# Making the low parts of the up weights on POOL instead of DVE, in an attention and feed-forward kernel

## The chip, the cores and the metric

The kernel runs on one core of one Trainium2 chip. The metric is device time in microseconds; lower is better. A core has several engines that work side by side, each on its own instructions in their order: PE (matmul), DVE, ACT and POOL (elementwise work), and SP (which here issues DMAs). They wait for each other through semaphores.

## The reference

Attention with a relative-position bias, then a gated feed-forward layer without a nonlinearity other than the product of its two up projections. Cut to what matters here:

```python
scores = scale * q @ k.T + bias            # B=8, H=8, S=576, D=64
attn = softmax(scores)
x = (attn @ v) -> (B*S, H*D)               # 4608 x 512

a = x @ w1                                 # 512 -> 1024, "up"
b = x @ w2                                 # 512 -> 1024, "up"
h = a * b @ w3                             # 1024 -> 1024
out = h @ w_out                            # 1024 -> 512
```

The feed-forward weights (w1, w2, w3, w_out) arrive as float64; the kernel sees them as pairs of 32-bit integers and makes float32 of them itself.

## The kernel before

**Split operands.** PE multiplies in a rounded format (fp32r). To keep accuracy, an operand is split into a high part, its rounded copy, and a low part, the difference of the operand and the high part. A product of two split operands is three matmuls: high by high, low by high, high by low. For the up weights the high part is `wh` (made by ACT, L579) and the low part is `wl` (made by DVE, L582).

**Stages.** First come a prologue (the bias table) and the attention, 32 units of one head pair and one batch each. In its last part, and overlapping its end, the kernel folds w3 and w_out into one matrix (`fold`, `evict_w`: L596 to L629). Then follow nine chunks of 512 tokens; in a chunk, eight steps `ft` of `up` (two groups of 12 matmuls, L661, into PSUM; ACT copies the first, DVE multiplies it with the second to `g`, ACT rounds it to `gh`, DVE makes `gl`) and `down` (12 matmuls with the folded matrix, L686). The up weights stay in SBUF for all chunks: they are made once.

**Up weights.** There are 16 tiles, for m = 0, 1 (w1, w2) and t = 0 to 7, each 128 x 512. This text numbers them n = 2t + m. `split_w` makes one, as a sequence of ten steps:

| step | line | engine | what |
|---|---|---|---|
| fetch | L123 | SP queue | DMA of the tile as integers to `wi` |
| size, rest | L128, L131 | ACT | `wmag` from the high words, `w` from the low words |
| clamp, shift, head, power | L134, L137, L143, L148 | DVE | bits of the float32 value in `wmag`, its power of two into `wi` |
| total | L151, L152 | POOL | `w` times the power, plus `wmag`: the float32 weight `w` |
| wh | L579 | ACT | the rounded copy |
| wl | L582 | DVE | `w` minus `wh` |

The pools give two buffers to `wi` and `wmag` and three to `w`, so the fetch of tile n + 2 waits until L151 of tile n has read its `wi`.

**Order.** The kernel writes the order of PE, ACT, DVE and POOL by hand: every step has a planned time, `drive` sorts the steps by it, and each engine gets its instructions in that order. Planned times are only keys for sorting. Tile n's steps stand at `AT_W1 + PACE_W * n` (4.0 and 5.7) after a base, plus the ten offsets in `AT_W`: total at +7.1, wh at +10.0, wl at +10.6. So on each engine wl of tile n stands between total of tile n and total of tile n + 1 (which is planned at +12.8).

```python
AT_W = 3.5, 0.0, 0.5, 1.2, 2.6, 3.8, 5.5, 7.1, 10.0, 10.6
```

**Neighbours in the same stretch.** The fold issues, for each of its 16 steps, an ACT rounding (`w3h`, L610), a DVE subtraction (`w3l`, L612) and 12 matmuls (L619); eight of the steps also have a POOL subtraction of the low part of w_out (L603, of the same form as wl: 128 x 512, fp32r from float32). `evict_w` has an ACT rounding and a DVE subtraction from PSUM (L626, L628). `split_x` splits the token chunk: DVE `xr` (L643), POOL `xh` (L647), DVE `xl` (L649). The first up steps bring DVE's `g` (L669, reads PSUM) and `gl` (L675). The up matmuls with `wl` (L661) of step t need both tiles n = 2t and n = 2t + 1.

Of the kernel before, what the change touches and what calls it, by code (L numbers as in the profile page):

```python
# [14 lines left out]
ALU = mybir.AluOpType  # L15
# [51 lines left out]
def relpos_attention_moe(  # L67
# [17 lines left out]
    nc = tc.nc  # L85
# [11 lines left out]
    def f(ap):  # L97
        return ap.bitcast(F32)
# [11 lines left out]
    def narrow(pool, src, n, x, queue, pieces=1):  # L110

        d = {}

        def cut(ap):
            return ap if pieces == 1 else ap.rearrange("p (c n) -> p c n", c=pieces)

        def fetch():
            if not WIDE:
                queue.dma_start(cut(x), src)
                return  # L120
            wi = pool.tile([P, n, 2], I32, name="wi")
            flat = wi.rearrange("p n t -> p (n t)")
            queue.dma_start(cut(flat), src.bitcast(I32))  # L123
            mag = pool.tile([P, n], F32, name="wmag")
            d.update(lo=wi[:, :, 0], hi=wi[:, :, 1], mag=mag, bits=mag.bitcast(I32), power=flat[:, 0:n])

        def size():
            nc.scalar.activation(d["mag"], f(d["hi"]), AF.Abs)  # L128

        def rest():  # L130
            nc.scalar.activation(x, d["lo"].bitcast(U32), AF.Copy, scale=2.0 ** -52)  # L131

        def clamp():
            nc.vector.tensor_scalar(d["mag"], d["mag"], LEAST, MOST, op0=ALU.max, op1=ALU.min)  # L134

        def shift():
            nc.vector.tensor_scalar(  # L137
                d["bits"], d["bits"], 3, 0x3FFFFFFF, op0=ALU.logical_shift_left, op1=ALU.bitwise_and,
            )

        def head():

            nc.vector.scalar_tensor_tensor(  # L143
                d["bits"], d["hi"], -0x40000000, d["bits"], op0=ALU.bitwise_and, op1=ALU.bitwise_or,
            )

        def power():
            nc.vector.tensor_scalar(d["power"], d["bits"], -0x800000, None, op0=ALU.bitwise_and)  # L148

        def total():  # L150
            nc.gpsimd.tensor_tensor(x, x, f(d["power"]), op=ALU.mult)  # L151
            nc.gpsimd.tensor_tensor(x, d["mag"], x, op=ALU.add)  # L152

        steps = [fetch, size, rest, clamp, shift, head, power, total]
        return steps if WIDE else [fetch] + [lambda: None] * 7
# [415 lines left out]
    def split_w(pool, t, m):  # L571
        src = (moe_w1, moe_w2)[m].rearrange("(c p) n -> p c n", p=P)[:, :, t * P:(t + 1) * P]
        w = cv.tile([P, NC * P], F32, name="w", bufs=3)
        for step in narrow(cv, src, NC * P, w, nc.sync, pieces=NC):
            step()
            yield
        w = w.rearrange("p (c n) -> p c n", c=NC)
        wh = pool.tile([P, NC, P], F32R, name=f"wh{m}{t}")
        nc.scalar.activation(wh, w, AF.Copy)  # L579
        yield  # L580
        wl = pool.tile([P, NC, P], F32R, name=f"wl{m}{t}")
        nc.vector.tensor_tensor(wl, w, f(wh), op=ALU.subtract)  # L582
        ups[m, t] = (wh, wl)

    def put_w(plan, pool, t, m, at):
        put(plan, split_w(pool, t, m), at - AT_W[0], *(at + d for d in AT_W[1:]))
# [149 lines left out]
    op = moe.enter_context(tc.tile_pool(name="op", bufs=NT))  # L736
# [73 lines left out]
```

## Time and profile before

| what | us |
|---|---|
| median of three runs (1241.46 to 1242.97) | 1242.62 |
| the profiled execution | 1243.18 |
| its span (first to last instruction) | 1241.4 |
| PE busy | 1200.8 |
| DVE busy | 656.6 |
| ACT busy | 603.5 |
| POOL busy | 390.0 |
| wl (L582), 16 instructions on DVE, starting from 603.7 to 702.9 | 11.3 |

The profile gives each instruction's engine, line, output and inputs, start and duration. Its views group instructions by line, list them in order of time, name what ended an engine's idle time (in brackets behind an instruction), and follow the chain that ended last back from the end. A duration is from an instruction's start on its engine to its end; where an instruction is held up after it has started, that shows as a longer duration, not as idle time. Starts of neighbours on DVE lie some 0.08 us closer than their durations say, since one begins while the one before it completes. The granted clock of PE is 0.989 over the span.

### The profile page before, as it was taken

The numbers are of one execution on the slowest core, as the hardware profiler recorded it, in microseconds if no ns is written. First come the engines' busy times: TensorE is split into PE (matmuls) and PEld (weight loads), VectorE is DVE, ScalarE is ACT, GpSimd is POOL, SyncE is SP. The second block draws the span as 40 slices with busy tenths as digits, with TensorE's granted clock in tenths as the row PEclk, the third lists the DMA queues.
The fourth block names the chain that finished last, engine by engine and source line by source line (L and its number), as shares of the span: only waits on it lengthen the run. The fifth ranks groups of instructions, "written<-read, shape, count | busy, mean of one in ns | idle before, by whom it ended". The sixth has DMA issues, their size and how long they took to land. (4 is left out here: it accounts for less than half of the span.)

```text
span 1241.4 us, 19015 instructions
## 1 busy us (share of the span) xinstructions
PE 1200.8 (97%) x7136; PEld 956.6 (77%) x7136; DVE 656.6 (53%) x1380; ACT 603.5 (49%) x1303; POOL 390.0 (31%) x260
## 2 busy tenths in 40 slices
PE   7679999999999999999989999999999999999998
PEld 3168887777778887887768788888888888888887
DVE  8647776777677767776999532222222131313111
ACT  7558887888788877888544321212121212121211
POOL 0436664666456655661654300000000000000000
PEclk9879999999999999999999999999999999999999
DMA  7854446444645463431443220212111110200001
GB/s 215 286 172 143 144 149 204 133 142 145 220 133 152 152 219 120 148 94 54 135 132 117 68 74 29 68 34 65 38 51 51 51 51 35 68 34 1 29 7 34
DMA packets 60795, 130.25 MB, mean 105 GB/s; under 512 B 8992, under 2 KB 18592, under 8 KB 60704
## 3 DMA queue, kind: packets, MB, share of 16 engines
q1 hardware_dynamic: 59408, 127.32, 32.7%
q10 hardware_dynamic: 1296, 1.72, 0.5%
q8 instruction: 56, 0.92, 0.3%
q14 instruction: 35, 0.29, 0.1%
HBM read 99.10 MB, written 29.92 MB: 104 GB/s over the span
## 5 line engine op out<-in xcount | busy, mean ns | idle before, releaser
L298 DVE CUSTOM_DVE_ANT_0 ts<-s,nb 128x576 f32<-128x576 f32 x256 | 184.7, 749 | 148.1 <-ACT pt L363 74.1
L661 PE MATMUL up<-xh,wl 128*128 128x512 f32 x576 | 225.4, 391 | 0.1
L669 DVE TENSOR_TENSOR g<-up,a 128x512 f32<-128x512 f32 x72 | 49.7, 690 | 332.2 <-PE up L661 332.2
L661 PE MATMUL up<-xh,wh 128*128 128x512 f32 x576 | 225.3, 391 | 0.0
L661 PE MATMUL up<-xl,wh 128*128 128x512 f32 x576 | 225.3, 391 | 0.0
L290 PE MATMUL s<-K,Q 128*128 128x288 f32 (+2 forms) x672 | 206.0, 326 | 16.2 <-DVE mx L298 7.6
L321 ACT ACTIVATE pp<-ts,mx 128x576 f32<-128x576 f32 x256 | 196.7, 770 | 39.2 <-DVE mx L298 39.1
L290 PE MATMUL s<-kl,Q 128*128 128x288 f32 (+2 forms) x672 | 182.1, 295 | 0.0
L686 PE MATMUL o<-w3s,gh 128*128 128x512 f32 x576 | 177.8, 390 | 0.0
L666 ACT COPY a<-up 128x512 f32<-128x512 f32 x72 | 42.2, 586 | 247.5 <-PE up L661 247.5
L647 POOL TENSOR_SCALAR xh<-xr 128x512 fp32r<-128x512 f32 x36 | 23.9, 664 | 435.7 <-DVE xr L643 432.5
L290 PEld LDWEIGHTS s<-K,Q 128*128 128x128 f32 x672 | 128.3, 191 | 38.2 <-DVE mx L298 18.0
L355 PE MATMUL pst<-ident,pp 128*128 128x128 f32 x1024 | 152.8, 278 | 0.0
L363 ACT ACTIVATE pt<-pst 128x512 f32<-128x512 f32 x224 | 129.5, 594 | 34.2 <-PE pst L355 29.9
L397 PE MATMUL pst<-pt,rv 128*64 128x320 f32 (+1 forms) x1024 | 138.3, 412 | 0.0
L355 PEld LDWEIGHTS pst<-ident,pp 128*128 128x128 f32 x1024 | 118.8, 141 | 15.2 <-DVE wi L148 11.8
L672 ACT ACTIVATE gh<-g 128x512 fp32r<-128x512 f32 x72 | 45.5, 632 | 172.8 <-DVE g L669 172.8
L290 PEld LDWEIGHTS s<-kl,Q 128*128 128x128 f32 x672 | 129.0, 192 | 0.0
L661 PEld LDWEIGHTS up<-xh,wl 128*128 128x128 f32 x576 | 108.2, 188 | 23.9 <-DVE wl L582 0.5
L661 PEld LDWEIGHTS up<-xl,wh 128*128 128x128 f32 x576 | 108.3, 188 | 23.3
L661 PEld LDWEIGHTS up<-xh,wh 128*128 128x128 f32 x576 | 108.3, 188 | 23.2
L686 PEld LDWEIGHTS o<-w3s,gh 128*128 128x128 f32 x576 | 108.2, 188 | 22.8
(85 smaller groups left out, 1720.3 us busy)
## 6 DMA issues: line engine op xcount, KB each, us to landing
rk<-in_k_dram SPq DMA_DIRECT2D x31, 576.0 KB
rq<-in_q_dram SPq DMA_DIRECT2D x31, 576.0 KB
wi<-in_moe_w_dram SPq DMA_DIRECT2D x32, 512.0 KB
nb_d<-bev SPq DMA_DIRECT2D x36, 295.5 KB
rv<-in_v_dram SPq DMA_DIRECT2D x32, 320.0 KB
x_d<-x SPq DMA_DIRECT2D x32, 288.0 KB
xr<-x_d SPq DMA_DIRECT2D x36, 256.0 KB
rb<-r_d SPq DMA_DIRECT2D x72, 128.0 KB
```

The costliest lines, as they stand in the source:

```text
L290: nc.tensor.matmul(o, l, r, start=(m == 0), stop=(m == len(ops) - 1))
L298: nc.vector.tensor_tensor_reduce(out=halves(ts), in0=d.pop(("s", t))[:, :, :HS], in1=halves(NB[p, t]), op0=ALU.add, op1=ALU.min, scale=-1. ...
L321: nc.scalar.activation(pp, ts, AF.Exp, bias=mx, scale=-1.0, accum_out=d["sum"][:, col:col + 1])
L355: nc.tensor.transpose(ps[:, c * P:(c + 1) * P], x, ident)
L363: nc.scalar.activation(o, x, AF.Copy)
L397: nc.tensor.matmul(acc[rows], x[:, c0:c0 + D], m, start=(c == 0), stop=(c == 4))
L647: nc.gpsimd.tensor_scalar(xh, xr, 1.0, 1.0, op0=ALU.mult, op1=ALU.mult)
L661: nc.tensor.matmul(acc, l[:, cc], r, start=(n == 0), stop=(n == 3 * NC - 1))
L666: nc.scalar.copy(a, ps[0])
L669: nc.vector.tensor_tensor(g, ps[1], a, op=ALU.mult)
L672: nc.scalar.activation(gh, g, AF.Copy)
L686: nc.tensor.matmul(d["o", t], l[:, sl], folded[ft][r], start=(ft == 0 and n == 0), stop=(ft == NF - 1 and n == 2),)
```

## The change

The subtraction that makes the low part of an up-weight tile is issued to POOL instead of DVE. Its planned time stays, so in POOL's order it stands behind total (L151, L152) of its own tile, and it waits there for ACT's `wh`.

```diff
@@ -579,7 +579,7 @@
         nc.scalar.activation(wh, w, AF.Copy)
         yield
         wl = pool.tile([P, NC, P], F32R, name=f"wl{m}{t}")
-        nc.vector.tensor_tensor(wl, w, f(wh), op=ALU.subtract)
+        nc.gpsimd.tensor_tensor(wl, w, f(wh), op=ALU.subtract)
         ups[m, t] = (wh, wl)
```

Nothing else is changed: tiles, buffers, planned times and the other engines' steps are the same.

## The prediction

> **What bounds the kernel now.** I read the page first, then the chain that ended last, then the stretch in which the edited line runs. The page: span, the busy tenths of DVE in 40 slices, and the chain by line.
>
> ```profile
> span 1241.4 us, 19015 instructions
> ...
> DVE  8647776777677767776999532222222131313111
> ...
> PE up L661 28%; PE o L686 14%; DVE wl L582 0%; DVE xr L643 0%; DVE wmag L143 0%; ACT osb L701 0%; DVE wmag L137 0%; POOL w L151 0%; POOL w L152 0%; ACT wh L579 0%; DVE gl L675 0%; DVE g L669 0%; ACTq L704 0%; ACT gh L672 0%; DVE xl L649 0%
> ```
>
> DVE reaches nine tenths in three slices only (about 590 to 683 us), and the chain that ended last, else PE's, passes through the small steps that prepare the up weights (wmag, w, wh, wl). The next view is that stretch, by windows (columns: length, then busy time and count of PE, PEld, DVE, ACT, POOL, then clock, DMA share, GB/s); the last row is the whole neighbourhood.
>
> ```profile
> 600.00:620.00 20.00, 19.73 (x90) 14.59 (x86) 19.90 (x22) 10.60 (x19) 13.22 (x10) 1.00 0.72 200
> 620.00:640.00 20.00, 15.59 (x64) 11.83 (x65) 19.96 (x27) 7.60 (x13) 10.10 (x8) 1.00 0.52 156
> 640.00:680.00 40.00, 40.00 (x176) 32.56 (x175) 39.01 (x51) 18.88 (x33) 19.72 (x15) 1.00 0.38 119
> 680.00:703.50 23.50, 22.64 (x99) 18.09 (x97) 18.76 (x28) 9.17 (x17) 12.49 (x10) 1.00 0.28 90
> 703.50:1241.40 537.90, 533.69 (x2340) 439.36 (x2339) 128.54 (x192) 96.69 (x166) 17.30 (x28) 1.00 0.13 42
> 590.00:720.00 130.00, 124.36 (x554) 97.55 (x553) 109.15 (x140) 56.63 (x100) 61.03 (x46) 1.00 0.38 116
> ```
>
> From 600 to 680 DVE is occupied 78.9 of 80 us. PE is idle 0.27 + 4.41 + 0 + 0.86 = 5.5 us between 600 and 703.5, and after that the kernel is PE alone for 537.9 us. So the end moves with the moment at which PE gets the last up weights. The chain around that moment, and, from the view of the waits between 580 and 760 us (total, times, longest), what PE waits for:
>
> ```profile
> 699.51 1.30 POOL w L151
> ...
> 702.85 0.70 DVE wl L582
> 703.55 0.04 issue
> 703.60 2.81 PE up L661 x11
> ```
> ```profile
> PE wacc L619 <- DVE w3l L612: 4.7, 3, 2.4
> ...
> PEld up L661 <- DVE wl L582: 0.5, 1, 0.5
> ```
>
> PE waits half a microsecond for the sixteenth low part, made at 702.85 to 703.55, and from there the chain is all PE but for the last output copy. There is therefore no slack at all: if the sixteen tiles come later, the end comes later by as much; if they come earlier, PE gains what it now idles, 5.5 us at the most.
>
> **The change: what goes from DVE.** Per tile one subtraction (L582). This is the tile numbered 5 of 0 to 15, in the timeline, ACT first, then POOL, then DVE:
>
> ```profile
> 641.41 0.63 ACT L579 ACTIVATE wh<-w 128x512 fp32r<-128x512 f32 x1 [2.81 <-POOL w L152]
> ```
> ```profile
> 644.06 1.30 POOL L151 TENSOR_TENSOR w<-w,wi 128x512 f32<-128x512 f32 x1 [2.68 <-issue]
> ```
> ```profile
> 641.69 0.69 DVE L143 SCALAR_TENSOR_TENSOR wmag<-wi,wmag 128x512 int32<-128x512 int32 x1
> 642.30 0.68 DVE L582 TENSOR_TENSOR wl<-w,wh 128x512 fp32r<-128x512 f32 x1
> 642.90 0.69 DVE L612 TENSOR_TENSOR w3l<-w3s,w3h 128x512 fp32r<-128x512 f32 x1
> 643.51 0.42 DVE L148 TENSOR_SCALAR wi<-wmag 128x512 int32<-128x512 int32 x1
> ```
>
> On a busy DVE the subtraction holds 642.90 - 642.30 = 0.60 us, so 16 of them give back 16 x 0.60 = 9.6 us of queue.
>
> **What comes to POOL, and what it does to DVE.** The kernel has POOL subtractions of the very same shape and types (L603). Here are two pairs of them in the same stretch, and the DVE instructions that lie beside them:
>
> ```profile
> 600.10 3.16 POOL L603 TENSOR_TENSOR wos<-wos,woh 128x512 fp32r<-128x512 f32 x2
> 607.89 3.18 POOL L603 TENSOR_TENSOR wos<-wos,woh 128x512 fp32r<-128x512 f32 x2
> ```
> ```profile
> 600.45 1.65 DVE L143 SCALAR_TENSOR_TENSOR wmag<-wi,wmag 128x512 int32<-128x512 int32 x1
> 602.03 1.78 DVE L612 TENSOR_TENSOR w3l<-w3s,w3h 128x512 fp32r<-128x512 f32 x1
> 608.14 1.78 DVE L612 TENSOR_TENSOR w3l<-w3s,w3h 128x512 fp32r<-128x512 f32 x1
> 609.85 1.77 DVE L143 SCALAR_TENSOR_TENSOR wmag<-wi,wmag 128x512 int32<-128x512 int32 x1
> ```
>
> Four POOL operations, four DVE operations of 1.65 to 1.78 us that take 0.68 to 0.69 us in the rows of tile 5, in POOL's idle 2.68 us. Each POOL subtraction cost DVE 0.97 to 1.10 us. That is more than the 0.60 us that leaves DVE. The groups of the whole stretch (590 to 720 us; count, busy time, mean ns) give the average, and show which operation does not suffer; the last row, one line's own view, gives the undisturbed time (minimum, median, maximum):
>
> ```profile
> L137 DVE TENSOR_SCALAR wmag<-wmag 128x512 int32<-128x512 int32 x16 | 17.0, 1063 | 0.3
> L134 DVE TENSOR_SCALAR wmag<-wmag 128x512 f32<-128x512 f32 x16 | 17.0, 1060 | 0.5 <-ACT wmag L128 0.5
> L143 DVE SCALAR_TENSOR_TENSOR wmag<-wi,wmag 128x512 int32<-128x512 int32 x16 | 15.7, 980 | 0.3
> L612 DVE TENSOR_TENSOR w3l<-w3s,w3h 128x512 fp32r<-128x512 f32 x15 | 15.1, 1003 | 1.6 <-ACT w3h L610 1.6
> L675 DVE TENSOR_TENSOR gl<-g,gh 128x512 fp32r<-128x512 f32 x9 | 9.3, 1037 | 2.0 <-ACT gh L672 1.8
> L669 DVE TENSOR_TENSOR g<-up,a 128x512 f32<-128x512 f32 x9 | 6.1, 682 | 8.6 <-PE up L661 8.6
> ```
> ```profile
> L134 DVE TENSOR_SCALAR wmag<-wmag x16: 414/1464/1524, 590.1 to 694.3; 128x512 f32<-128x512 f32 x16
> ```
>
> Over 0.41 us for L134 and L137 and 0.68 for the others, the excess is 16 x 0.65 + 16 x 0.65 + 16 x 0.30 + 15 x 0.32 + 9 x 0.36 = 33.6 us, beside 46 POOL operations (the count in the last window row): 0.73 us each on average (xh operations, which are shorter, among them). g, which reads one operand from PSUM, stays at 0.68 us. So the stall falls on DVE instructions with both inputs in SBUF and on the short tensor-scalar ones, and only while POOL works.
>
> The Trainium skill, page "SBUF — State Buffer", section "Who interferes with whom", speaks against the change: VectorE and GpSimd arbitrate for one pair of SBUF ports, and it is an exclusive lock held for the whole instruction. The rows above agree on which instructions suffer. Taken to the letter it would charge a whole POOL operation of about 1.28 us per tile, an estimate of 16 x (1.28 - 0.60) = 10.9 us; the rows show 0.2 to 0.3 us less per operation.
>
> **Where the POOL step stands.** In POOL's order it comes after its own tile's L152 and before the next tile's L151, a few times with an xh (L647) beside it. It waits for ACT's wh. In tile 5, wh ends at 642.04 and POOL has nothing until 644.06: a 1.3 us operation fits, so POOL's time as such is covered. Its port isn't. Step by step: POOL gets in when DVE's L143 is done (about 642.3) and holds to 643.6; w3l, next on DVE, is held off and ends near 644.2; L148 follows, near 644.55; L151 of the next tile, which needs L148, starts near 644.65 instead of 644.06. Shift: +0.6, against 1.10 - 0.60 = 0.50 by the rule of the rows. Behind the waiting wl stand L151, L152 and, in some tiles, xh on POOL, and through them ACT's wh, DVE's xl (which needs xh), and the weight fetch of two tiles on, since SP waits for L151 to free the buffer:
>
> ```profile
> SPq L123 <- POOL w L151: 56.3, 13, 7.5
> ```
>
> So the shift stays in the loop and is carried on. The tile w, now freed by POOL, has three buffers, so ACT needs it back three tiles later; that costs nothing. No DMA is issued by the moved step. I went through the timeline for the other tiles in this way. In twelve of the first fifteen the DVE instruction due when wh is ready is L148, w3l, xr, xl, L137 or a gl: price 0.50 each, 6.0 us. In three (tiles 2, 3 and 8) POOL meets evictions from PSUM, g, or a DVE that waits for xh anyway: I take 0.1 each, 0.3 us. The sixteenth has no successor; it lies itself on the chain, and takes about 1.3 us (L151 took 1.30 there) instead of 0.70: 0.6 us.
>
> **Sum.** 6.0 + 0.3 + 0.6 = 6.9, taken as +7 us. Bounds: with the average of 0.73 for all, 16 x 0.13 + 0.6 = 2.7 us; with 1.10 for all, 16 x 0.50 + 0.6 = 8.6 us. I stand near the upper one because the rows that are the same operation (L603) are those of 0.97 to 1.10. PE's present gaps do not cover it: 4.7 of the 5.5 us are waits for DVE's own w3l, which comes later too. The profiled execution took 1243.18 us, 1.8 more than its span; the median of the three runs is 1242.62. 1242.6 + 7 = 1249.6 us.
>
> **Rivals.**
>
> *DVE is really relieved (faster).* If POOL's operation mostly found DVE in PSUM work, or let DVE pass, a lock would cost less than 0.60 us, and below that the sign turns. At no cost DVE would be 9.6 us earlier, less 0.6 for the last tile; PE can take only the 5.5 us of its idle time, so 1237 us. For it: DVE is the fuller engine, and the new POOL step falls in POOL's idle time. Against it: the four L603 rows. The Trainium skill, page "Perfetto Trace Analysis", section "Optimizing Scalar/DVE Operations", says that moving work off a saturated DVE, even to GPSIMD, may make sense, and adds that for these two it might not help. Chance 0.10.
>
> *A wash.* A price near 0.60 to 0.7 us, the gain in the queue paid back by the lock: 1242 to 1245 us. The average of 0.73 lies close by. Chance 0.12 within 0.2% (2.5 us, about what a measurement of this kernel tells from no change), and 0.13 for a small loss of 2.5 to 4.5 us.
>
> *POOL's own queue becomes the bound.* Means of the rows in this stretch:
>
> ```profile
> L151 POOL TENSOR_TENSOR w<-w,wi 128x512 f32<-128x512 f32 x16 | 23.4, 1463 | 36.5 <-ACT w L131 17.7 <-issue 7.1 <-DVE wi L148 4.2
> ```
>
> L151 at 1.46, L152 of the same form at as much, ACT's 0.7 between, and the subtraction at 1.58 (half of 3.16) make 5.2 us a tile; from tile 5 to 15 the pitch of L151 is (699.51 - 644.06) / 10 = 5.5 us. It holds on average, with 0.3 us to spare, but xh and the pairs of L603 stand in the same queue. If this bites in half of the tiles by 0.5 us, 4 us come on top: 1253 to 1255 us. Chance 0.10.
>
> The forecast, 1247 to 1252, has the rest, 0.55. Slower by over 0.2%: 0.55 + 0.13 + 0.10 = 0.78; the same 0.12; faster 0.10. The range leaves a tenth on each side: 1242.5, which takes in the wash and the low bound, to 1254.5.
>
> **What would show it.** Right: wl on POOL sixteen times at 1.3 to 1.6 us; DVE's L148, now 0.42 us in tile 5, and w3l longer by about 1 us in most tiles; the last wl ending near 710 instead of 703.5; PE's idle time before it up by 7 us; the stretch behind it 538 us as before. Wrong: L148 still at 0.4 us and DVE with gaps (the relief), or DVE idle while POOL works back to back (POOL's queue). What would make the number wrong is above all the order in which the two engines get in: I assume that POOL waits for one DVE instruction and no more.

## The result: slower by half a per cent

| | kernel before | changed kernel |
|---|---|---|
| median of four runs each, us | 1242.75 (1241.46 to 1242.97) | 1248.80 (1248.24 to 1250.01) |
| the profiled execution, us | 1243.18 | 1249.16 |
| its span, us | 1241.4 | 1247.2 |

The ratio is 1.0052 [1.0037, 1.0067], a loss of 6.05 us. The forecast was +7 us, 1249.6 us.

**The page after.** The span, the busy tenths of DVE and of POOL in 40 slices of about 31 us:

```profile
span 1247.2 us, 19031 instructions
...
DVE  8647776777677767775989622222212231313111
...
POOL 0436664666466655661766500000000000000000
```

DVE is still in its eights and nines between 590 and 690 us, although sixteen instructions have left it: what the subtraction gave back was taken up again.

**The stretch before the last up weights**, in the windows view (length, then busy time and count of PE, PEld, DVE, ACT, POOL, then clock, DMA share, GB/s); the last row is again 590 to 720:

```profile
600.00:620.00 20.00, 18.99 (x84) 13.94 (x79) 19.90 (x18) 9.80 (x18) 16.93 (x12) 1.00 0.70 193
620.00:640.00 20.00, 15.37 (x56) 11.43 (x57) 18.75 (x24) 6.37 (x11) 12.22 (x10) 0.91 0.46 148
640.00:680.00 40.00, 39.81 (x174) 32.27 (x173) 35.24 (x40) 18.37 (x32) 28.60 (x22) 1.00 0.32 100
680.00:703.50 23.50, 21.09 (x90) 16.02 (x89) 21.47 (x26) 9.30 (x16) 15.76 (x13) 1.00 0.38 122
590.00:720.00 130.00, 120.76 (x521) 92.64 (x520) 108.39 (x120) 53.46 (x95) 84.70 (x62) 0.99 0.35 108
```

In the 130 us of the last row DVE runs 120 instructions instead of 140, yet is occupied 108.39 us instead of 109.15. POOL goes from 61.03 to 84.70 us. PE loses: 521 matmuls in place of 554.

**The chain around the last up weights**, from the view of the chain that ended last (start, duration):

```profile
703.25 1.41 DVE wi L148
...
704.73 1.30 POOL w L151
...
706.10 1.29 POOL w L152
...
707.41 0.64 ACT wh L579
...
708.12 1.28 POOL wl L582
...
709.45 2.79 PE up L661 x11
```

PE begins its unbroken run at 709.45 instead of 703.60. From there to the end of the span it is 1247.2 - 709.45 = 537.75 us, before 1241.4 - 703.60 = 537.8: nothing behind the last tile has changed, and the whole loss lies ahead of it. The first row also shows what happened to L148: 1.41 us for an instruction that took 0.42 in the forecast's tile 5.

**The groups of DVE** in the same 130 us (count, busy time, mean ns, then idle time before them and what ended it), of the changed kernel, the two that grew most and the one that waits most:

```profile
L612 DVE TENSOR_TENSOR w3l<-w3s,w3h 128x512 fp32r<-128x512 f32 x14 | 15.1, 1078 | 5.0 <-ACT w3h L610 5.0
...
L148 DVE TENSOR_SCALAR wi<-wmag 128x512 int32<-128x512 int32 x16 | 12.8, 802 | 0.3
L649 DVE TENSOR_TENSOR xl<-xr,xh 128x512 fp32r<-128x512 f32 x8 | 11.0, 1379 | 2.8 <-POOL xh L647 2.8
```

and of the kernel before:

```profile
L148 DVE TENSOR_SCALAR wi<-wmag 128x512 int32<-128x512 int32 x16 | 7.1, 444 | 0.0
L649 DVE TENSOR_TENSOR xl<-xr,xh 128x512 fp32r<-128x512 f32 x8 | 6.5, 815 | 1.8 <-POOL xh L647 1.8
```

L148 took 444 ns and xl 815 before; now L148 takes 802 ns on average and xl 1379. These two are often the instruction that stands next on DVE when wh is ready and POOL starts on wl. Together they are 5.7 + 4.5 = 10.2 us longer, against the 11.3 us of the wl group that left DVE. L134 and L137 went the other way: they stood at 1060 and 1063 ns and are now at 963 and 950.

**A wait that the forecast did not have.** L612 waits 5.0 us for ACT, before 1.6. Three quarters of it is one instruction, in DVE's timeline of the changed kernel (idle time and its releaser in brackets):

```profile
643.24 1.37 DVE L612 TENSOR_TENSOR w3l<-w3s,w3h 128x512 fp32r<-128x512 f32 x1 [3.74 <-ACT w3h L610]
```

ACT's timeline there, of the changed kernel and then of the kernel before:

```profile
642.06 0.63 ACT L579 ACTIVATE wh<-w 128x512 fp32r<-128x512 f32 x1 [4.50 <-POOL w L152]
642.59 0.62 ACT L610 ACTIVATE w3h<-w3s 128x512 fp32r<-128x512 f32 x1
643.11 0.66 ACT L128 ACTIVATE wmag<-wi 128x512 f32<-128x512 f32 x1
```
```profile
635.67 0.63 ACT L579 ACTIVATE wh<-w 128x512 fp32r<-128x512 f32 x1 [5.27 <-POOL w L152]
636.21 1.14 ACT L610 ACTIVATE w3h<-w3s 128x512 fp32r<-128x512 f32 x2
637.36 0.68 ACT L128 ACTIVATE wmag<-wi 128x512 f32<-128x512 f32 x1
637.94 0.66 ACT L131 ACTIVATE w<-wi 128x512 f32<-128x512 uint32 x1
```

Before, ACT had done two w3h and then L128 and L131 of tile 6 by 638.6, ahead of the wh of tile 5 (641.41). After, wh of tile 5 and a w3h came first, and L128 of tile 6 behind them. DVE's order differs there too: its L134, L137 and L143 of tile 6, which ran from 638.70 to 642.38 before, now stand behind this w3l, so DVE has nothing to do while ACT waits 4.50 us for POOL's L152 of tile 5. So three more things differ than the diff says: ACT and DVE have another order at one place, and DVE stands idle there. The place is the seam at which the program passes from one planned list (`later`) to the next (`plan`); tile 6 (4.0 + 5.7 x 6 = 38.2, against a limit of 46.8 - 10.0) is the first of the second list. Five early up matmuls of PE also moved behind matmuls of the fold. Why the compiled order differs there although the planned times are the same, the trace does not tell. This had to be separated from the cost of the moved step: that is what the fourth and fifth experiments do.

### The profile page after: what moved, and what is told of

Read it like the earlier page. It is cut to its first block, busy times and chain, and to the rows that moved or that the text cites. A ratio compares the mean times of both kernels' runs of the same rounds, so it can differ in the third digit from the quotient of the medians.

```text
span 1247.2 us, 19031 instructions
## 1 busy us (share of the span) xinstructions
PE 1203.0 (96%) x7136; PEld 956.5 (77%) x7136; DVE 657.7 (53%) x1364; ACT 602.9 (48%) x1303; POOL 413.3 (33%) x276
## 4 chain that ended last, share of the span: by engine, by line
PE 75%; DVE 11%; DMA 2%; ACT 2%; POOL 2%; issue 1%; SPq 0%; ACTq 0%; DVEq 0%; POOLq 0%
PE up L661 28%; PE o L686 14%; PE pst L397 13%; PE s L290 11%; PE pst L355 5%; DVE r L328 4%; DVE ts L298 3%; PE wacc L619 2%; ACT pt L363 1%; DMA nbM<-nb_d 1%; POOL w L151 1%; DVE px L361 1%; DMA rb<-r_d 1%; DMA wi<-in_moe_w_dram 1%; DVE wi L148 0%
## 5 line engine op out<-in xcount | busy, mean ns | idle before, releaser
L669 DVE TENSOR_TENSOR g<-up,a 128x512 f32<-128x512 f32 x72 | 49.7, 691 | 332.2 <-PE up L661 332.2
```

The source lines that it names most:

```text
L669: nc.vector.tensor_tensor(g, ps[1], a, op=ALU.mult)
```

## The experiments

Two theories stood at first (a third, POOL's own queue, is among the rivals further down). **The lock**: POOL's operation holds up DVE's by more than the 0.60 us that left DVE; the loss then grows with each reading POOL operation and needs no change of order. **The order**: the subtraction costs nothing much; the loss is the seam's wait and what moved with it. All ratios are against the kernel before, run beside it on the same chip, with their 95% intervals.

### 1. No low parts at all, one constant tile

The subtraction is left out; all up matmuls with wl read one tile that is set once.

```diff
+    const_wl = w01.tile([P, NC, P], F32R, name="const_wl")
+    nc.gpsimd.memset(f(const_wl), 1e-4)
...
-        wl = pool.tile([P, NC, P], F32R, name=f"wl{m}{t}")
-        nc.vector.tensor_tensor(wl, w, f(wh), op=ALU.subtract)
-        ups[m, t] = (wh, wl)
+        ups[m, t] = (wh, const_wl)
```

> The low parts of the up weights are not made at all: every tile uses one constant tile in their place, so PE multiplies as often, and no engine does the 16 subtractions. Every engine's other instructions stand in the order of the changed kernel. It prices the POOL subtraction in that order, and what the freed DVE time alone is worth. Lock theory (each POOL subtraction holds up DVE by about 0.8 to 1.1 us, and DVE sets when the last up weight is ready): 9.6 us of DVE queue gone and no new lock, so 3 to 5.5 us below the kernel before (PE idled 5.5 us), 1237 to 1240 us, and about 10 us below the changed kernel. Theory that POOL's own queue delays the changed kernel, DVE being no bound: no more than 1 us below the kernel before. Theory that the changed order of the other engines, not the POOL work, makes the loss: 3 us or more above the kernel before.

Measured: 1249.18 us, 1.0055 [1.0041, 1.0068], +6.4 us. The number is what the order theory expected, 3 us or more above the kernel before, and far from the 1237 to 1240 us of the lock. It has another cause, which the chain after the last tile shows:

```profile
714.76 5.61 PE up L661 x24
720.38 2.75 PE o L686 x12
723.12 5.58 PE up L661 x24
...
731.45 5.58 PE up L661 x24
```

The same stretch of the kernel before:

```profile
714.75 2.75 PE o L686 x12
717.49 5.61 PE up L661 x24
...
725.85 5.44 PE up L661 x24
731.29 2.72 PE o L686 x12
```

Before, 24 up matmuls take 5.61 us in the first two steps of a chunk, whose weights lie in the pool `w01`, and 5.44 in the other six, whose weights lie in `wpool`. With the constant tile in `w01` they take 5.58 to 5.61 in all of them. So the experiment had changed PE's pace behind the stretch: with 0.14 us in each of 6 x 9 steps and 0.03 for each `down`, some 9 us. It says nothing on either theory until the tile is put elsewhere.

### 2. The same, with a constant tile in each pool

```diff
+        ups[m, t] = (wh, const_wl[0] if t < 2 else const_wl[1])
```

`const_wl[0]` lies in `w01`, `const_wl[1]` in `wpool`; else as experiment 1.

> The same question as e1_no_wl: the low parts of the up weights are not made, constant tiles stand in their place, every engine's other instructions are in the order of the changed kernel. In e1_no_wl all low parts were one tile beside those of the first two up steps, and its trace shows PE taking 5.58 us for each pair of up groups where the kernel before takes 5.44 us in six steps of eight (and 5.61 us in the two whose weights lie there). Here the constant tile of the other six steps lies where the kernel before has their weights. Lock theory: 3 to 5.5 us below the kernel before, 1237 to 1240 us, so 9 to 12 us below the changed kernel. Theory that the order or PE, and not the subtraction, makes the loss: 1248 us or more again.

Measured: 1239.76 us, 0.9976 [0.9966, 0.9986], -2.7 us. The time is in the lock's range; the gain is just short of the 3 us at its lower end. With each taken against the kernel before beside it, experiment 2 lies 6.4 + 2.7 = 9.1 us below experiment 1, from which it differs only in where the constant low parts lie. Without any subtraction the kernel is 6.05 + 2.7 = 8.8 us below the changed kernel, with the same order on ACT and DVE, and on PE behind the prologue: that is what sixteen subtractions on POOL cost in all. The seam's wait is in this kernel too (DVE's group in the 130 us), so the wait and the orders do not by themselves make a kernel slower than the one before:

```profile
L612 DVE TENSOR_TENSOR w3l<-w3s,w3h 128x512 fp32r<-128x512 f32 x14 | 13.4, 955 | 5.2 <-ACT w3h L610 5.2
```

What the wait costs when DVE is the late one, this kernel cannot tell. Its L669 waits 19.9 us for PE in these 130 us (8.6 in the kernel before, 2.4 in the changed one), so its DVE has time to spare.

### 3. The subtraction on DVE, and again on POOL

POOL's copy writes a scratch tile that nobody reads. In this stretch every other instruction stands where it stood in the kernel before, on PE, ACT, DVE and POOL, so the order theory has nothing to act on.

```diff
         ups[m, t] = (wh, wl)
+        scr = cv.tile([P, NC, P], F32R, name="scr", bufs=1)
+        nc.gpsimd.tensor_tensor(scr, w, f(wh), op=ALU.subtract)
```

> The kernel before, with DVE making the low parts as it did, and POOL doing the same 16 subtractions once more into a scratch tile that nobody reads, at the place where the changed kernel has them. All other instructions are in the order of the kernel before on every engine. So nothing is taken from DVE and POOL's work is added alone. Lock theory: 16 times 0.8 to 1.1 us on DVE's queue, 13 to 17 us slower than before, 1255 to 1260 us, with DVE busy longer but doing the same work. Theory of POOL's queue or of the order: POOL's operation fits in its idle time, so at most 2 us slower, 1243 to 1245 us.

Measured: 1257.71 us, 1.0122 [1.0108, 1.0135], +15.0 us. The lock's number; the order alone would have given none. The stretch from the first L151 of tile 0 to the end of the last wl, in the windows view, before and here:

```profile
597.04:703.54 106.50, 100.92 (x439) 79.02 (x437) 100.60 (x127) 46.39 (x82) 58.41 (x44) 1.00 0.44 132
```
```profile
594.97:716.46 121.49, 106.58 (x439) 80.45 (x437) 115.98 (x127) 46.28 (x82) 82.76 (x60) 0.97 0.38 115
```

The counts of PE, DVE and ACT are the same (439, 127, 82), POOL has sixteen more. The stretch is 15.0 us longer, and DVE is busy 15.38 us longer with the same 127 instructions. 15.38 / 16 = 0.96 us per POOL operation: the lock's price, with no order changed.

### 4 and 5. The seam moved, in the changed kernel and in the kernel before

One number decides which tiles go into which planned list. With 8.0 tile 6 goes into the first, and both kernels get one and the same ACT order, and DVE's differs by wl alone. On PE the five moved up matmuls still stand differently in the two, as in the original pair; experiment 2 has them where the changed kernel has them, and is faster than the kernel before.

```diff
-        put_w(later if at < t_f - 10.0 else plan, wpool, n // 2, n % 2, at)
+        put_w(later if at < t_f - 8.0 else plan, wpool, n // 2, n % 2, at)
```

The changed kernel with it:

> The changed kernel with one more tile (number 6) planned together with the tiles before it instead of with those after it. In the changed kernel ACT's and DVE's first steps of tile 6 had moved behind the last steps of the fold, which the kernel before does not have; here they are back ahead of them. To be compared with e5_seam_before, which has the same regrouping and the same order on ACT and (but for the moved subtraction) on DVE. Lock theory: 6 to 8 us above e5_seam_before, 1248 to 1251 us. If the order at tile 6 is a good part of the loss: only 2 to 4 us above e5_seam_before.

The kernel before with it:

> The kernel before with tile 6 planned together with the tiles before it, low parts on DVE: the partner of e4_seam_after. All theories: within 1.5 us of the kernel before, 1241 to 1244 us, as DVE has the same work in nearly the same order.

Measured: 1247.62 us, 1.0042 [1.0029, 1.0054], +4.9 us, and 1241.55 us, 0.9990 [0.9981, 0.9999], -1.2 us. The first lies 0.4 us below its expected range, the second in it. The difference is 6.07 us, within the expected 6 to 8 and as large as that of the original pair (6.05). Moving the seam is worth 1.2 us in either kernel, so, within intervals of some 2 us, it explains none of the loss. The same stretch of wl on POOL, then of wl on DVE:

```profile
595.81:707.85 112.04, 104.76 (x439) 81.15 (x437) 104.19 (x111) 46.84 (x82) 82.16 (x60) 0.97 0.41 125
```
```profile
594.74:700.40 105.66, 102.42 (x439) 80.07 (x437) 98.99 (x127) 46.49 (x82) 58.63 (x44) 0.98 0.45 133
```

112.04 - 105.66 = 6.4 us longer. DVE has sixteen instructions fewer and is busy 5.20 us more; with the 16 x 0.60 = 9.6 us that left it, POOL has cost it 14.8 us, 0.93 per operation. Only 6.4 - 5.2 = 1.2 us is DVE standing idle.

### 6. POOL as busy, but only writing

A memset of about the same length (1258 ns) in place of experiment 3's extra subtraction. It tells whether POOL's occupation or its reading is what counts.

```diff
+        scr = cv.tile([P, 1344], F32, name="scr", bufs=1)
+        nc.gpsimd.memset(scr, 0.0)
```

> Like e2_both (the kernel before, and 16 POOL operations added at the same place in POOL's order), but the added operation fills a scratch tile of 128 x 1344 with zeros: it occupies POOL for about as long and writes SBUF, but reads nothing and waits for nothing. Lock theory, by the reading side (DVE's two-input operations are held up by POOL operations that read SBUF): far below the 15 us of e2_both, at most 4 us, 1243 to 1247 us. Theory that POOL's occupied queue is what costs: as e2_both, 1255 us or more. If any POOL access to SBUF holds DVE up: between, near e2_both.

Measured: 1246.20 us, 1.0030 [1.0020, 1.0040], +3.7 us, a quarter of experiment 3's. POOL's and DVE's groups in the 130 us:

```profile
L585 POOL MEMSET scr<- 128x1344 f32 x16 | 20.1, 1258 | 0.0
```
```profile
L137 DVE TENSOR_SCALAR wmag<-wmag 128x512 int32<-128x512 int32 x16 | 20.9, 1304 | 0.3
...
L143 DVE SCALAR_TENSOR_TENSOR wmag<-wi,wmag 128x512 int32<-128x512 int32 x16 | 15.7, 979 | 0.3
```

L143, with two inputs in SBUF, takes 979 ns where it took 980 before. In four tiles it ran wholly beside a memset, and took 0.68 to 0.69 us there: a POOL that only writes does not hold it. L137, one input and constants, goes from 1063 to 1304 ns, 3.9 us in all, as much as the whole loss; three of the sixteen take 2.55 to 2.56 us, where they took 1.39 to 1.41. The Trainium skill, page "SBUF — State Buffer", section "Who interferes with whom", has this split: a VectorE operation with two SBUF inputs contends with a GpSimd operation that reads SBUF and not with one that only writes it, while one in a two-port mode, which a tensor-scalar operation can enter, contends with GpSimd without that limit. The two rows agree; that L137 ran in such a mode, no run shows.

### 7 to 10. The reverse

If a reading POOL operation costs DVE 0.93 to 0.96 us and doing it on DVE costs 0.60, then the 32 reading operations that POOL already has (L151, L152) should be better on DVE, until PE's idle time of 5.5 us is used up.

```diff
-            nc.gpsimd.tensor_tensor(x, x, f(d["power"]), op=ALU.mult)
-            nc.gpsimd.tensor_tensor(x, d["mag"], x, op=ALU.add)
+            on = (nc.gpsimd, nc.gpsimd) if pieces == 1 else (nc.vector, nc.vector)
+            on[0].tensor_tensor(x, x, f(d["power"]), op=ALU.mult)
+            on[1].tensor_tensor(x, d["mag"], x, op=ALU.add)
```

Experiment 7, both steps of total on DVE, wl on DVE:

> The kernel before with the other two POOL steps of the up weights (the product and the sum, L151 and L152, of these 16 tiles alone) moved to DVE as well: the change turned round. Lock theory: 32 x 0.60 = 19 us more on DVE's queue, and 32 locks of 0.7 to 1.1 us gone (22 to 35 us), so DVE is earlier by 3 to 16 us, of which PE can use what it idled, 5.5 us: 1237 to 1241 us. Theory that the fuller engine should be relieved: 10 us or more slower, 1253 to 1262 us.

Experiment 8, only the addition (L152) on DVE, that is (nc.gpsimd, nc.vector) in the pair:

> Half of e6_total_dve: of the two POOL steps of the up weights only the sum (L152) goes to DVE, the product (L151) stays on POOL. Lock theory, with a lock near 0.9 us and 0.60 us for the step on DVE: 16 x 0.3 = 5 us earlier on DVE's queue, so between the kernel before and e6_total_dve, 1238 to 1241 us. If instead each POOL operation cost DVE less than 0.60 us: 1243 us or more.

Experiment 9, both steps of total on DVE and wl on POOL, the changed kernel with experiment 7's edit:

> The changed kernel (low parts on POOL) with the product and the sum of these 16 tiles on DVE: POOL does 16 operations for the up weights instead of 48, DVE two more per tile than in the changed kernel. Lock theory: what counts is how many reading POOL operations lie in the stretch, not which. Against the kernel before DVE has 16 x 0.60 = 9.6 us more work and 16 locks of about 0.9 us less, so 1238 to 1242 us, 7 us or more below the changed kernel. Theory that the subtraction itself is a bad step to move (it waits for ACT in POOL's queue and lies last in each tile's chain): no better than the changed kernel, 1248 us or more.

Experiment 10, as 7, with the fold's low part (L603) on DVE as well:

> e6_total_dve with the eight subtractions of the fold (L603) on DVE too; only the xh rounding is left on POOL in this stretch. Lock theory: 8 locks of about 1.1 us against 8 x 0.60 us, so DVE 2 to 4 us earlier in the first part of the stretch, but PE has only 2.1 us of idle time left between 590 and 720 us in e6_total_dve: 1235.5 to 1238 us. Otherwise slower than e6_total_dve by up to 5 us.

| experiment | reading operations of 128x512 on POOL per up-weight tile | us | ratio |
|---|---|---|---|
| changed kernel | 3 | 1248.80 | 1.0052 [1.0037, 1.0067] |
| kernel before | 2 | 1242.75 | 1 |
| 8, addition on DVE | 1 | 1238.37 | 0.9971 [0.9960, 0.9983] |
| 9, total on DVE, wl on POOL | 1 | 1240.74 | 0.9991 [0.9982, 1.0000] |
| 7, total and wl on DVE | 0 | 1237.18 | 0.9959 [0.9946, 0.9971] |
| 10, as 7 with L603 | 0 | 1240.71 | 0.9994 [0.9985, 1.0003] |

Experiment 7 beats both kernels: 5.3 us below the one before, and so 5.3 + 6.05 = 11.3 below the changed one. Its 130 us, and three of DVE's groups in them:

```profile
590.00:720.00 130.00, 127.91 (x573) 101.21 (x572) 101.79 (x173) 57.69 (x102) 15.31 (x14) 1.00 0.38 116
```
```profile
L143 DVE SCALAR_TENSOR_TENSOR wmag<-wi,wmag 128x512 int32<-128x512 int32 x16 | 12.7, 791 | 0.2
...
L134 DVE TENSOR_SCALAR wmag<-wmag 128x512 f32<-128x512 f32 x16 | 8.0, 499 | 3.9 <-ACT wmag L128 3.6
L137 DVE TENSOR_SCALAR wmag<-wmag 128x512 int32<-128x512 int32 x16 | 7.8, 488 | 0.0
```

DVE runs 173 instructions instead of 140 and is busy 101.79 us instead of 109.15. L134 and L137 fall from 1060 ns to 499 and 488. PE now idles 130 - 127.91 = 2.1 us, so little is left to win.

Experiment 9 came out as expected and 1.1 + 6.05 = 7.2 us below the changed kernel, but 2.4 above experiment 8, with as many reading operations on POOL. In it the operation that POOL keeps waits for ACT and is the last of the tile, and some of PE's early up matmuls stand elsewhere; which of these is why was not tried. Experiment 10 missed the lock's range by 2.7 us and came out in the other case of its expectation: with L603 on DVE as well the gain is 1.2 us, not clear of none, where experiment 7 has 5.3. DVE's timeline there, and the first place in the 130 us where PE waits:

```profile
591.60 0.69 DVE L604 TENSOR_TENSOR wos<-wos,woh 128x512 fp32r<-128x512 f32 x1 [0.89 <-ACT woh L600]
```
```profile
616.74 0.50 PE L620 MATMUL wacc<-woh,w3h 128*128 128x512 f32 x1 [1.76 <-ACT w3h L611]
```

DVE's queue now stands behind ACT's rounding of w_out, and PE waits 1.76 us for a w3h. Whether the one leads to the other stays open. DVE is no longer what is late there: it is busy only 97.86 of the 130 us, and stands idle for 7.80 us at 615.64 until ACT has done an L128. The simple rule "fewer reading POOL operations are faster" is clear from three to two per up-weight tile, and from two to one in experiment 8; from one to none (experiments 8 and 7) the intervals overlap, experiment 9 with one is not clear of the kernel before, and for L603 the rule fails.

### 11. The weights' addresses

Eight float32 per partition, put ahead of `w01`, shift that pool's start by 32 bytes, in case the slower pace of the first two steps comes from where it begins.

```diff
+    padp = moe.enter_context(tc.tile_pool(name="padp", bufs=1, side="right"))
+    pad = padp.tile([P, 8], F32, name="pad")
+    nc.gpsimd.memset(pad, 0.0)
     w01 = moe.enter_context(tc.tile_pool(name="w01", bufs=1, side="right"))
```

> The kernel before with a tile of 32 bytes per partition put ahead of the pool that holds the up weights of the first two steps. Without it these eight tiles start 32 bytes off a multiple of 64 bytes, while the weights of the other six steps start at multiples of 64. In every trace so far the first two steps of a chunk take PE 5.61 and 2.75 us, the other six 5.44 and 2.72. If the address makes it: 18 of 72 steps get 0.20 us shorter, 3.6 us less, 1238.5 to 1240 us, and the slow pairs are gone. If something else marks these steps: no change, 1241.5 to 1243.5 us.

Measured: 1241.92 us, 0.9997 [0.9988, 1.0006]. The steps with weights in `w01` still take longer than the next ones, in the chain:

```profile
714.75 5.60 PE up L664 x24
720.35 2.75 PE o L689 x12
723.10 5.44 PE up L664 x24
```

The idea falls; that the pace goes with the pool is shown, why it does is not.

## Why the forecast was right, point by point

**What bounds the kernel: right.** No slack behind the last tile (537.75 against 537.8 us), so each microsecond of lateness showed at the end: last wl later by 709.40 - 703.55 = 5.85 us, span longer by 5.8, profiled execution by 1249.16 - 1243.18 = 5.98. The last wl ended at 709.4, forecast near 710.

**The sign: right, and for the reason given.** A POOL subtraction costs DVE more than DVE's own. Experiments 3 and 4/5 measured 0.96 and 0.93 us per operation against 0.60, with the order of ACT and DVE held, in experiment 3 that of PE too. The changed kernel's own rows say the same. In fourteen of the first fifteen tiles one DVE instruction stays unfinished until wl on POOL has ended, and ends 0.28 to 0.29 us (L148, L137) or 0.55 us (two inputs) after it; this is tile 7:

```profile
656.77 1.30 POOL L582 TENSOR_TENSOR wl<-w,wh 128x512 fp32r<-128x512 f32 x1 [2.24 <-ACT wh L579]
```
```profile
656.81 1.54 DVE L148 TENSOR_SCALAR wi<-wmag 128x512 int32<-128x512 int32 x1
```

These fourteen are longer than undisturbed (0.41 or 0.68 us) by 0.48 to 1.13 us, 13.6 us in all, 0.91 per tile: each by what was left of wl when its turn came, less 0.13 to 0.14 us.

The forecast took 1.10 for twelve tiles, from rows that said 0.97 to 1.10, and nearly nothing for tiles 2, 3 and 8. Fourteen were held, at 13.6 / 14 = 0.97 us; tiles 2, 3 and 8 by 0.48, 1.08 and 0.83, and the one that met only evictions was tile 6. So the price per held tile was a little too high and the number of held tiles too low, and it is partly luck that the two balance. The term of 6.3 us for fifteen tiles measured 15 x (0.93 - 0.60) = 5.0 by experiments 4/5; with 0.6 for the sixteenth, which lies itself on the chain (1.28 instead of 0.70), that is 5.6 us where the forecast had 6.9. The interval of the result, 4.6 to 8.3 us, would hold either sum. The average of 0.73 was too low as a price, since it counts operations that met nothing.

The Trainium skill, page "SBUF — State Buffer", section "Who interferes with whom", taken to the letter (a whole POOL operation per tile, the estimate of 10.9 us), is above that interval. The held instruction does wait for POOL's end, but its turn comes after POOL has started, so an operation of 1.27 us or more cost DVE 0.93 to 0.96 on average.

**How it is made up in the changed kernel: not as forecast.** The stretch from the first L151 to the last wl:

```profile
596.06:709.39 113.33, 104.14 (x439) 79.70 (x437) 101.77 (x111) 46.40 (x82) 82.07 (x60) 0.98 0.40 124
```

It is 113.33 - 106.50 = 6.8 us longer than before (it began 1.0 us earlier; in the other kernels it began at 594.7 to 595.8, so the start is not the edit's). Of these 6.8, DVE's busy time grew by 101.77 - 100.60 = 1.2 us only, and its idle time by 5.7. The forecast had it all as DVE's queue. In experiments 4/5, with one order on ACT and DVE, the same loss is 5.2 us of busy time and 1.2 us idle. In the changed kernel the seam puts a 3.74 us wait on DVE, and while DVE stands idle POOL's operations hold up nothing (L134 and L137, at 963 and 950 ns, are held less than before); so the one replaces the other and the sum stays. That last step is argued from the two ledgers. That the seam adds nothing to the loss rests on the equal differences (6.05 and 6.07), within the 2 us of their intervals. The forecast did not see the seam, and owes it to luck that the seam left the sum alone.

**PE's idle time: half right.** The forecast had 7 us more. From 600 to 703.5 it is 1.01 + 4.63 + 0.19 + 2.41 = 8.2 us, and 1.0 more from 703.5 to 710, by this row:

```profile
703.50:710.00 6.50, 5.50 (x23) 4.01 (x22) 3.09 (x3) 1.62 (x3) 4.71 (x4) 1.00 0.00 0
```

9.2 against 5.5 us: 3.7 more. The rest is not idle time: over the stretch PE is busy 104.14 us with the same 439 matmuls that took 100.92 before, at a granted clock of 0.98, with 0.91 between 620 and 640. The lower clock is also in experiments 3, 4 and 5 (0.97, 0.97, 0.98), the last of which is not slower than the kernel before; what sets it was not tried.

**The rows that were to show it.** wl on POOL:

```profile
L582 POOL TENSOR_TENSOR wl<-w,wh x16: 1272/1464/1746, 602.2 to 708.1; 128x512 fp32r<-128x512 f32 x16
```

1.27 to 1.75 us, forecast 1.3 to 1.6. L148 is longer by 802 - 444 = 358 ns on average, held in six tiles by 0.83 to 1.13 us; in eight others it was w3l, xr, xl or L137 that stood next. Which instruction pays was less sure than that one does.

**The rivals.** Relief needed a lock below 0.60 us, and the measured 0.93 to 0.96 excludes it. The wash needed a price near 0.60 to 0.7 us; the same runs exclude it, and the loss of 6.05 us lies outside it. POOL's own queue: its two groups of the 130 us with idle time ahead of them,

```profile
L582 POOL TENSOR_TENSOR wl<-w,wh 128x512 fp32r<-128x512 f32 x16 | 23.7, 1483 | 10.2 <-ACT wh L579 10.2
L151 POOL TENSOR_TENSOR w<-w,wi 128x512 f32<-128x512 f32 x16 | 23.6, 1477 | 13.4 <-DVE wi L148 13.4
```

show that POOL still stands idle for 10.2 and 13.4 us until ACT and DVE have done their steps, and experiment 6, with POOL occupied nearly as long, costs a quarter of experiment 3. That memset also waits for nothing, unlike wl; but in experiment 3, where POOL's operation does wait for wh, the 15.0 us are all in the durations of DVE's instructions (15.38), not in idle time of DVE. POOL's queue does not bound the kernel.

## What to carry to other kernels

Before work is moved from a full DVE to an idle POOL, look in the trace for DVE instructions that lie beside POOL operations of the same form, and set their excess against what the move saves: here 0.93 to 0.96 us were paid for 0.60. The idle time of POOL is no measure of what it may take, and the cheaper kernel came from the reverse move, up to the idle time that the bounding engine had left. When an experiment is to show one cost, look first whether its instruction order and the places of its tiles are those of the kernel that it is compared with.

## What was not expected of the hardware

The pace of PE depends on where its stationary tiles lie. With the low parts of the up weights in `wpool` 24 up matmuls take 5.44 us, with them in `w01` 5.58 to 5.61, and 5.58 even where the high parts stay in `wpool`. Experiment 2, whose last six steps share one tile in `wpool`, has 5.44 again, so sharing a tile is not it. Between experiments 1 and 2 the place of one 128x512 tile is worth 9.1 us of 1240, more than the whole change. Experiment 11 excludes a start shifted by 32 bytes as the cure, and no run tells the cause.

DVE can be less busy with more to do: with 33 instructions more in the 130 us, the DVE of experiment 7 was busy 7.4 us less.
